# Queries and keys of the first four blocks as plain fp32 copies in a fused attention and MLP kernel on one Trainium2 core

## The chip, the core and the metric

The kernel runs on one core of a Trainium2 chip. A core has five engines that run their own instruction streams in order and wait for each other through semaphores: TensorE (PE, matrix products and transposes), VectorE (DVE), ScalarE (ACT), GpSimd (POOL) and SyncE (SP, which here only starts transfers). Sixteen DMA engines move data between main memory (HBM) and on-chip memory (SBUF). PE writes into PSUM, a small memory of eight banks, from which DVE or ACT must fetch the result. The metric is the device time of one execution in microseconds (us).

## What is computed

The first half is attention with four "sink" positions and a window of 128 positions; the second half is an MLP with a sigmoid gate on the attention's output. Shapes: 4 batches, 8 heads, 768 positions, 64 numbers per head; the MLP goes 512 to 2048 to 512 for 3072 tokens.

```
scores = scale * q @ k.T                         # per batch and head
keep   = (pos_k < 4) | (0 <= pos_q - pos_k < 128)
a      = softmax(where(keep, scores, -1e9))
x      = (a @ v) as (3072, 512)
h      = x @ w_in
out    = (h * sigmoid(1.702 * h)) @ w_out
```

## The kernel before, in words

The 3072 tokens are 24 blocks of 128 positions, six per batch. Blocks are worked in the order 0, 6, 12, 18 (the first block of every batch), then 1, 2, 3, 4, 5, 7 and so on. The number behind an operation's name is its block (or, for the MLP, its group: groups 0 and 1 are blocks 0 and 6 alone, group 2 is blocks 12 and 18, group 3 is blocks 1 and 2, and from there on two blocks each).

**Attention of a block.** `k0`, `q0`, `v0` load the block. For the first eight blocks q and k land as 128 rows of 512 numbers in the tile `qkn`. PE transposes them (`tk`, `tq`), DVE or ACT copies the result from PSUM into `qkT` (`ck`, `cq`). PE forms the scores in two PSUM tiles (`sc`; in the first block of a batch after a mask, `msk`, which is itself a product with the constant `identb`; in the others with the sink scores `snk`). DVE takes the row maxima (`mx`). In the first four blocks DVE negates them (`nb`) and ACT takes the exponential straight from PSUM (`bx`, eight instructions per block); in the others DVE masks and subtracts (`pk`, `sb`) and ACT takes the exponential from SBUF (`ex`). The result is transposed, for the first six blocks by PE (`ta`, fetched by `ca`) and from then on by a DMA transpose on SP's queue (`tat`); POOL cuts the window out of it (`sp`, `so`); PE multiplies with the values (`av`), DVE divides by the sums (`nm`). The block's output is transposed by PE (`tx`, fetched by `cx`) or by a DMA transpose (`txd`).

**MLP of a group.** `h3_0` to `h3_7` are the products with `w_in`, one PSUM tile each; the gate follows on ACT (`g`), or for groups 0 to 2 as a tanh on ACT (`th`) and a multiplication on DVE (`g`). `o1_0` to `o1_3` are the four quarters of the product with `w_out` for block 1; quarter n needs the n-th quarter `wo0` to `wo3` of `w_out`, as the n-th quarter of the `h` needs `wi0` to `wi3` of `w_in`. `ev` fetches and `st` stores the block's output.

**What sets the order.** Every operation is recorded with the engines that may run it, the operations it depends on and the buffers it takes and frees. The string `ORDER` then gives one order of all operations, by number; a letter behind a number picks the engine where there is a choice (d for DVE, a for ACT, p for POOL, s for SP). Each engine runs its operations in that order, one after the other, so an instruction that waits holds up everything behind it on its engine. Buffers are rings: `mm` (three PSUM tiles) serves `tk`, `tq`, `ta`, `tx`, `h` and `o`; `sc` (two PSUM tiles) one block's scores. A transfer carries a semaphore out of one of two rings of eight, one for transfers started by POOL and one for those started by SP and ACT together, and a transfer waits, on the engine that starts it, until the transfer that had the same semaphore eight places before it has landed.

**The transfers.** Before the change all q, k, v and weight loads are started by POOL (lines L286, L294, L263, L300, L307); these convert fp32 to fp16 on the way. SP and ACT start only the constants (L215), the four small loads `vsa0` to `vsa3` of the sink values (L315, used by `vsb0` to `vsb3`, L320), the DMA transposes and the stores. The tail of the kernel is block 23, whose output is split into 320 and 192 columns.

The beginning of each engine's order before the change:

```
PE   msk0 tk0 tq0 tk6 sc0 tk12 tq12 ta0_0 tq6 msk6 av0_0 ta0_1 sc6 tq2 av0_1 tk18 tx0 ta6_0 tq18 h0_3 ...
ACT  own bias0 later ck0 cq0 ck6 ck12 bx0_0 bx0_1 cq6 ca0_1 cq2 bx6_0 bx6_1 cq18 th0_3 ca6_1 th0_0 ...
DVE  zv zk z1 za1 za2 za3 zs za0 vsb0 vsb1 ks0 mx0_0 vsb3 nb0_0 mx0_1 nb0_1 cq12 ca0_0 ...
POOL k0 q0 k6 k12 v0 q12 q6 q2 wi3 k18 vsb2 v6 q18 wi0 wi1 k1 wi2 v12 wo0 wo1 q1 v18 wo2 wo3 k4 k2 q4 ...
SP   ident bias1 identb vsa0 vsa1 vsa2 vsa3 st0 st6 ...
```

Of the kernel before, what the change touches and what calls it, by code (L numbers as in the profile page):

```python
# [11 lines left out]
FP32 = mybir.dt.float32  # L12
# [7 lines left out]
P = 128  # L20
D = 64
# [3 lines left out]
PE, ACT, DVE, POOL, SP = "PE", "ACT", "DVE", "POOL", "SP"  # L25
BLOCKS = [0, 6, 12, 18] + [6 * s + r for s in range(4) for r in range(1, 6)]
# [4 lines left out]
TQ = {0, 6, 12, 18}  # L31
# [23 lines left out]
108 106 126a 99p 148 109 101d 149a 19 110 112 111 24 113 150 114 86 115 151d 127 88 116d 130 128a 152 26 129 119 117  # L55
90 120 131 118a 227 132 22 121 228a 135 133 122 171 87 134 136 123 172d 89 137 138 124d 173 27 139d 619 174a 175 153
25 620 142 621 140 154 143 141a 610 158 155 91 144 613 611 145 612 146 614 93 159 147d 194 160 156 615 631 195d 157
637 35 632 616 29 638 633 176 639 617 161 628 618 162a 36 634 629 177 630 635 163 181 622 164a 636 34 167 182 640 178
183 168 623 32 179 180 196 33 641 197d 165 184 166 198 38 185a 624 204 201 188 186 189 642 187a 28 625 190 169 626a
191 643 43 170a 627 199 192 644a 37 200 280 193d 225 645 281a 202 39 652 226a 205 40 282 653 230 203 658 31 283a 231  # L60
208 207 649 654 41 659 206 285 210 258 42 650 660 229 259a 651 256 209 232 211 257a 646 286 212a 233 215 261 647 655
213 235 216a 648 214 304 661 656 234 217 657 670 239 218 236 662 664 44 262 238 671 45 237 241 665 663 219 240 46 260
666 242 220 672 243a 263 221 266 244 246 667 222 247a 245 267 306 248 676 323 668 307 249 268 250 677 669 49 251 673
47 264 252 674a 48 678 265 675 269 253 284 270 223 287 254 224a 679 271 290 255a 288 344 680a 682 291 681 692 683 289
688 345 292 325 293 689 305 326 693 684 308 294 311 686 309 272 690 312 687 273 295 310 313 276 50 314 324 277 685 696
51 691 327 315 330 52 704 328 694 331 296 705 697 329 316 333 274 297 332 706 275 695 55 343 361 334 300 349 54 278
698 301 53 346 298 699 350 317 279a 335 347 707 318 299 700 708a 352 348 302 709 58 701 351 303a 56 353 722 702d 57
712 703 723 354 718 319 713 362 399 320 719 720 368 336 365 321 721 714 322 337 710 715 61 363 724 711 364 60 369 340
725 732 341 59 370 716 366 338 717 726 355 367 371 733 339 372 356 342 382 381 383 734 384 64 387 727 373 63 385 357
62 388 728 419 386 735 389 729 736a 390 358 391 742 737 730d 401 392 746 743 402 359 400 731 360 374 748 747 403 406  # L70
740 375 749 404 738 741 407 67 744 739 405 66 408 376 745 750 65 377 409 754 410 378 760 393 379 420 380 751 761 394
426 423 421 755 70 411 422 427 762 68 424 752 69 457 428 395 753 425 756 396 763 429 430 757 764d 439 412 765 766 758d
440 759 774 767 413 431 397 768 398 71 495 775 438 72 769 770 441 73 444 776 771 442 416 777 445 772 417 778 773 447
446 414 779 443 780 432 415 448 788 418 433 477 782 478 789 75 781 449 783 74 459 790 76 460 784 791 796 792a 458 793
797 800 461 450 464 798 801 462 451 794 514 799 465 806 79 463 795 466 802 77 807 467 468 454 78 476 455 810 482 479
452 803 811 469 483 785 453 480 434 786a 808 484 787 485 804 435 809 481 497 816 805 498 486 436 496 437 470 812 499
456 502 516 817 471 500 813 487 503 81 818 517 814a 82 505 501 474 815 819 504 80 475 506 830 820d 822 507 831 826 821
488 472 823 515 473 827 832 521 489 518 836 833 522 85 824 837 519 83 552 828 825 523 84 520 490 829 834 508 491 524
534 525 492 509 537 838 493 844 540 494 835 535 839 536 538 512 526 845 541 840 539 542 846 590 513 841 543 544 847
842d 510 843 527 848d 860 511 849 850 528 861 545 573 553 574 864 559 851 556 852 865 531 853 856 532 872 857 546 554  # L80
854 555 547 557 529 855 858 530 558 866 533 859 560 862 561 867 863 562 563 572 868 575 578 548 873 576 564 579 869
577 874 870a 580 892 871 581 549 582 875 893 583 550 876d 591 565 551 886 877 597 566 882 594 887 592 880 883 593 598
567 881 888 584 568 595 878 889 585 599 569 879 884 596 570 894 885 600 571 601 900 895 890 602 896 891 901 586 902
587 916 897 603 917 910 898a 604 588 899 911 912 589 903 913 906 904a 607 905 907 914 608 908 915 918 909 922 919 605
928 606 920 609 929 921 923 930 924 931 925 932a 946 933 926a 934 927 947 944 935 940 945 938 941 936 939 948 937 962
949 950 942 951 943 956 952 957 953 958 954a 963 959 955 964 960a 965 961 966a 967
"""


# [64 lines left out]
def kernel(  # L154
# [12 lines left out]
    Bsz, H, S, Dh = q.shape  # L167
# [20 lines left out]
    def sb(tag, shape, dt, name):  # L188
        return Buf(tag, lambda: work.tile(list(shape), dt, tag=tag, bufs=RING[tag], name=name))
# [20 lines left out]
    def queue(e):  # L210
        return nc.scalar if e == ACT else nc.sync
# [21 lines left out]
    def copy(e, dst, src, factor=1.0):  # L233
        if e == POOL:
            nc.gpsimd.tensor_copy(out=dst, in_=src)
        elif e == DVE and factor != 1.0:
            nc.vector.tensor_scalar(out=dst, in0=src, scalar1=factor, scalar2=None, op0=ALU.mult)
        elif e == DVE:
            nc.vector.tensor_copy(out=dst, in_=src)
        elif factor != 1.0:  # L240
            nc.scalar.mul(out=dst, in_=src, mul=factor)
        else:
            nc.scalar.copy(out=dst, in_=src)  # L243
# [8 lines left out]
    for unit in XUNITS:  # L252
        buf = sb("xn", (P, max(map(len, XUNITS)), H, D), FP16, f"xn{unit[0]}")
        for n, b in enumerate(unit):
            xunit[b] = (buf, n, unit)

    for pos, b in enumerate(BLOCKS):
        bb, r = divmod(b, 6)
        for w, src in (("k", k), ("q", q), ("v", v)):
            view = src[bb, :, r * P : (r + 1) * P, :].rearrange("h s d -> s h d")  # L260
            if w == "v":
                ld["v", b] = plan.add(
                    f"v{b}", POOL, 0.88, lambda b=b, view=view: nc.gpsimd.dma_start(v65[:, b, :, 0:D], view),  # L263
                    deps=[z_1], dma=("ld", LD), key=10 * pos - 45,
                )
            else:
                buf, n, unit = tunit[b]
                if b in HW:
# [583 lines left out]
```

## Time and profile before

| what | value |
|---|---|
| median of 3 runs | 234.83 us (234.34 to 236.19) |
| the profiled execution, whole | 235.92 us |
| its span, first to last instruction | 234.2 us |
| granted TensorE clock | 1.00 of full speed |
| PE busy | 218.3 us (93%) |
| DVE, ACT, POOL busy | 148.6, 146.1, 110.5 us |
| loads started by POOL | 13.64 MB as written, 66816 packets |
| first `h` product, last quarter of `w_out` in use | 19.70 us, 39.78 us |

The span leaves out 1.7 us of the execution's time. Busy time of PE is an upper bound of its work, because the ends of matmuls are modelled and a matmul that is held up inside the pipeline counts as busy. In the profile "L739" is line 739 of the kernel; a name such as `hT` is a tile. `PEld` is PE's load of weights, which runs beside the products. `ACTq` and `SPq` are the engines' queues for starting transfers.

### The profile page before, as it was taken

Reading aid. Unit: us, or ns where it says so; the run is one execution under the profiler, and the core shown is the slowest. Engines: PE = TensorE matmul, PEld = TensorE weight load, DVE = VectorE, ACT = ScalarE, POOL = GpSimd, SP = SyncE. Lnnn points to the kernel's source line nnn. Section 1 sums busy time; section 2 is a strip of 40 time slices with the busy share of each in tenths; the row PEclk is TensorE's granted clock in tenths of the full one; section 3 lists DMA queues with packets and bytes.
Section 4 is the critical chain, followed back from the end, with each engine's and each line's share of the span. In section 5 each row is a group of like instructions: output and inputs, shape, how many; then the busy total and the mean of one; then the engine's idle time right before and its main releaser. Section 6 shows DMA issues by size and latency. Waiting matters only on the chain.

```text
span 234.2 us, 5547 instructions
## 1 busy us (share of the span) xinstructions
PE 218.3 (93%) x2250; PEld 152.2 (65%) x2250; DVE 148.6 (63%) x384; ACT 146.1 (62%) x226; POOL 110.5 (47%) x129
## 2 busy tenths in 40 slices
PE   0778899999998999999999799999999999999994
PEld 0556865776585478576587486586586585775863
DVE  2587765899999967876966079869857782210000
ACT  2368663885599884477488368578474668351632
POOL 8594433966435958764950880838312060300000
PEclk9999999999999999999999999999999999999999
DMA  5999999999989999999999999699982534412202
GB/s 83 181 158 199 195 197 192 196 147 108 174 112 119 114 171 182 169 182 188 173 132 192 159 145 191 91 201 167 163 143 45 98 95 68 75 45 48 90 0 90
DMA packets 117832, 32.08 MB, mean 137 GB/s; under 512 B 108432, under 2 KB 114864, under 8 KB 117808
## 3 DMA queue, kind: packets, MB, share of 16 engines
q0 software_dynamic: 66816, 13.64, 69.6%
q1 hardware_dynamic: 50656, 18.00, 45.0%
q8 instruction: 17, 0.28, 0.5%
q10 hardware_dynamic: 336, 0.10, 0.2%
q14 instruction: 7, 0.06, 0.1%
HBM read 27.46 MB, written 6.29 MB: 144 GB/s over the span
## 4 chain that ended last, share of the span: by engine, by line
PE 63%; DVE 16%; DMA 16%; POOL 2%; issue 1%; SPq 0%; ACT 0%; DVEq 0%
PE hT L739 27%; PE o L789 27%; DMA w_out<-in_moe_w_out_dram 6%; DMA w_in<-in_moe_w_in_dram 4%; DVE mx L498 3%; DMA xT<-xn 3%; DVE e L535 3%; PE sc L436 3%; DVE sc L488 3%; DVE gT L760 2%; DMA vsa<-in_v_dram 2%; PE av L663 2%; PE av L665 2%; PE av L658 2%; DVE xn L676 1%; DVE mx L501 1%
## 5 line engine op out<-in xcount | busy, mean ns | idle before, releaser
L739 PE MATMUL hT<-xT,w_in 128*128 128x256 f16 (+1 forms) x832 | 93.2, 264 | 2.6 <-DMA xT<-xn 1.2
L789 PE MATMUL o<-w_out,gT 128*128 128x512 f16 (+2 forms) x400 | 91.9, 370 | 0.5 <-DMA w_out<-in_moe_w_out_dram 0.4
L739 PEld LDWEIGHTS <-w_in 128*128 128x128 f16 x832 | 73.8, 98 | 16.4 <-issue 4.3
L769 ACT ACTIVATE gT<-hT 128x512 f16<-128x512 f32 x80 | 46.5, 597 | 31.5 <-PE hT L739 31.3
L789 PEld LDWEIGHTS <-gT 128*128 128x128 f16 x400 | 36.4, 97 | 33.4 <-issue 1.9
L590 POOL TENSOR_SCALAR_AFFINE_SELECT atp<-at 128x1024 f16<-128x1024 f16 (+1 forms) x22 | 22.2, 1010 | 74.5 <-DMA at<-a 62.3
L498 DVE TENSOR_REDUCE mx<-sc 128x4 f32<-128x512 f32 x48 | 32.5, 681 | 0.1
L488 DVE COPY_PREDICATED sc<-later,sc 128x512 f32<-128x512 uint16 x40 | 26.0, 689 | 7.4 <-PE sc L436 7.1
L535 DVE TENSOR_TENSOR e<-sc,mx 128x512 f32<-128x512 f32 x40 | 26.3, 681 | 0.1
L675 DVE RECIPROCAL rcp<-av 128x4 f32<-128x4 f32 x48 | 8.5, 176 | 27.3 <-PE av L665 24.3
L559 ACT ACTIVATE a<-e 128x1056 f16<-128x1056 f32 (+2 forms) x24 | 22.5, 938 | 4.2 <-DVE rcp L675 1.6
L263 POOL DMA_DIRECT2D v<-in_v_dram x24 | 21.7, 906 | 6.1 <-DMA w_out<-in_moe_w_out_dram 3.3
L590 POOL TENSOR_SCALAR_AFFINE_SELECT at<-at 128x1024 f16<-128x1024 f16 (+1 forms) x22 | 22.2, 1010 | 1.5
L676 DVE TENSOR_TENSOR xn<-av,rcp 128x256 f16<-128x256 f32 x48 | 20.4, 424 | 1.7
L559 ACT ACT_TABLE_LOAD x13 | 16.7, 1283 | 5.7 <-issue 3.1
L769 ACT ACT_TABLE_LOAD x14 | 18.0, 1283 | 1.1 <-PE hT L739 0.5
L243 ACT COPY osb<-o 128x512 f32<-128x512 f32 (+2 forms) x13 | 7.2, 553 | 18.3 <-PE o L789 14.1
L663 PE MATMUL av<-v,at 128*128 128x65 f16 x192 | 17.5, 195 | 0.3 <-POOL at L590 0.3
L663 PEld LDWEIGHTS <-at 128*128 128x128 f16 x192 | 14.7, 99 | 4.1 <-POOL at L590 0.6
L294 POOL DMA_DIRECT2D qkn<-in_k_dram x16 | 14.4, 897 | 2.1 <-PE sc L436 2.1
L665 PE MATMUL av<-v,atp 128*128 128x65 f16 x160 | 15.1, 194 | 0.0
L294 POOL DMA_DIRECT2D qkn<-in_q_dram x16 | 14.3, 894 | 0.0
(54 smaller groups left out, 197.2 us busy)
## 6 DMA issues: line engine op xcount, KB each, us to landing
out_dram<-osb SPq DMA_DIRECT2D x23, 256.0 KB, 4.0
qkn<-in_k_dram POOLq DMA_DIRECT2D x24, 128.0 KB, 6.9
qkn<-in_q_dram POOLq DMA_DIRECT2D x24, 128.0 KB, 6.5
v<-in_v_dram POOLq DMA_DIRECT2D x24, 128.0 KB, 6.7
w_in<-in_moe_w_in_dram POOLq DMA_DIRECT2D x4, 512.0 KB, 9.1
w_out<-in_moe_w_out_dram POOLq DMA_DIRECT2D x4, 512.0 KB, 13.9
at<-a SPq DMA_TRANSPOSE x18, 5.2
qkT<-qkn SPq DMA_TRANSPOSE x10, 6.3
```

What stands on the lines that cost most here:

```text
L263: f"v{b}", POOL, 0.88, lambda b=b, view=view: nc.gpsimd.dma_start(v65[:, b, :, 0:D], view),
L294: lambda buf=buf, n=n, w=w, view=view: nc.gpsimd.dma_start(buf()[:, n, "qk".index(w)], view),
L488: nc.vector.copy_predicated(out=t()[:, :, :, own].rearrange("p l j s -> p (l j) s"), mask=later.unsqueeze(1).to_broadcast((P, 4, P)), data ...
L498: nc.vector.tensor_reduce(out=part, in_=t()[:, :, :, own], axis=AX.X, op=ALU.max)
L535: nc.vector.tensor_tensor(out=e32()[:, 512 * hf : 512 * hf + 512].rearrange("p (l j s) -> p l j s", l=2, j=2), in0=t()[:, :, :, own], in1= ...
L559: nc.scalar.activation(out=a16()[:, lo:hi], in_=e32()[:, lo:hi], func=AF.Exp, scale=scale)
L590: nc.gpsimd.affine_select(out=dst, in_=at()[:, lo : lo + num], pattern=[[0, num], [1 if own else -1, P]], compare_op=ALU.is_ge if own else ...
L663: nc.tensor.matmul(av()[:, i], at()[:, c], v65[:, b, h], start=(r == 0), stop=(r == 0))
L676: nc.vector.tensor_tensor(out=xn()[:, xi, 4 * hf : 4 * hf + 4].rearrange("p (j l) d -> p l j d", l=2), in0=av()[:, :, 0:D].rearrange("p (l ...
L739: nc.tensor.matmul(ht()[:, n].rearrange("p (n t) -> p n t", n=NT), w_in16[:, c, bass.ts(f, P)], t0()[:, i0 : i0 + NT, c], start=(c == 0), ...
L769: lambda fs=fs, gt=gt, ht=ht: nc.scalar.activation(out=gt()[:, fs[0] : fs[-1] + 1], in_=ht(), func=AF.Gelu_apprx_sigmoid),
L789: nc.tensor.matmul(po()[:, 0:width], gt()[:, F, bass.ts(t, P)], w_out16[:, F, c0 : c0 + width], start=(F == 0), stop=(F == NF - 1),)
```

## The change

Queries and keys of blocks 0, 6, 12 and 18 no longer come through POOL. Each of these eight loads becomes two operations. `rk6` (say) is a plain fp32 copy of the same 256 KB, started by SP or ACT, into a quarter of a tile of the ring `gt2` (two tiles, of which the MLP's groups 3 to 12 later hold their gates); `fk6` then converts it to fp16 into `qkn`, on DVE, ACT or POOL. The ring of `qkn` grows from four to seven tiles. The string `ORDER` is a new one, over 976 operations where there were 968.

```diff
+HW = {0,6,12,18}
+LH = 0.64
+RING = dict(RING,qkn=7)
 ORDER = """
-4a 8d 1s 14 2s 0a 6 7 5s 3a 11 15 12 13 9 10 94 17 96 20 16 98 100 107 21 18 102 95d 30 103a 104 97d 92 105a 125 23
...
+19a 13 5s 12 10 11 38 1s 9 21a 7 31s 8d 34 0a 14s 6 29a 94 106 16a 23 4s 20d 2a 104 133 100 26a 22d 24s 134d 3a 135 35
...
+    raws = {}
+    for n, b in enumerate(b for b in BLOCKS if b in HW):
+        if n % 2 == 0:
+            buf = sb("gt2", (P, 4, H * D), FP32, f"raw{n // 2}")
+        raws[b] = (buf, 2 * (n % 2))
...
+                    if b in HW:
+                        raw, ri = raws[b]
+                        ri += w == "k"
+                        o = plan.add(
+                            f"r{w}{b}", {SP: 0.6, ACT: 0.65}, 0,
+                            lambda e, raw=raw, ri=ri, view=view: queue(e).dma_start(raw()[:, ri], view),
+                            take=[raw], dma=("h", LH), key=10 * pos - 2000,
+                        )
+                        ld[w, b] = plan.add(
+                            f"f{w}{b}", {DVE: 0.4, ACT: 0.49, POOL: 0.9}, 0,
+                            lambda e, buf=buf, n=n, w=w, raw=raw, ri=ri: copy(
+                                e, buf()[:, n, "qk".index(w)].rearrange("p t d -> p (t d)"), raw()[:, ri]
+                            ),
+                            deps=[o], take=[buf], give=[raw], key=10 * pos - 500,
+                        )
+                        continue
```

The new order moves more than the eight loads. Block 6 now comes first; the beginning of each engine's order is

```
PE   tk6 tq6 msk6 tq18 sc6 tk0 tq2 tk18 tk1 tq0 ta6_1 msk0 ta6_0 sc0 tq12 av6_0 av6_1 tk12 ta0_1 tx6 msk12 ta0_0 sc12 h1_0
     av0_0 h1_3 tq1 av0_1 h1_2 ta12_0 snk1 msk18 tx0 sc18 h1_1 ta12_1 h0_2 av12_1 h0_0 h0_1 av12_0 o6_0 sc1 ta18_0 o6_1 tk2
     h0_3 snk2 o0_0 o6_2 o0_1 av18_0 sc2 ta1_1 o0_2 ta1_0 o6_3 o0_3 ...
ACT  rk6 rq6 bias0 rk18 rq0 bias1 rq12 later cq6 cq18 ck0 cq2 bx6_1 bx6_0 fq12 ca6_1 cq12 bx0_1 bx0_0 cx6 ca0_0 ca0_1 th1_0
     bx12_0 bx12_1 th1_3 th1_2 cx0 th1_1 bx18_1 th0_2 bx18_0 th0_0 th0_1 ca18_0 ck2 th0_3 ex1_1 ...
DVE  za3 za2 za0 za1 zs z1 zv zk fk6 fq6 ck6 fq18 fk0 ks6 fk18 mx6_1 mx6_0 nb6_1 fq0 nb6_0 ck1 ck18 cq0 ks18 ks0 ca6_0 mx0_1 ...
POOL q2 k1 wi0 v6 wi3 q1 v0 wi2 wi1 v12 vsb2 wo0 vsb1 k2 fk12 wo1 wo2 k3 v18 wo3 q3 k5 q4 k4 ...
SP   identb ident rq18 rk0 vsa2 own vsa1 rk12 vsa0 vsa3 st6 st0 ...
```

In this order the semaphores of SP's and ACT's transfers come round as follows: `vsa2` waits for `rk6`, `rq0` for `identb`, `bias1` for `rq18`, `rq12` for `rk0`, `rk12` for `bias0`, and `later`, the last transfer that ACT starts before its first computation, for `vsa2`. In the output of block 23 the wider part (320 columns) is now the last product.

More of the change, by code (lines that the diff above doesn't have):

```diff
@@ L58 @@
[L58 to L62, printed above, removed]
@@ new lines @@
+238 630 628 36 239 650 214 211 217 631 39 215 216 629 196 218 237 51 197 223 243 632 224a 240 48 219 244 651 220a 225
+241 633 652a 221 245 194 653 49 634a 264 246 195d 248 266 635 242 50 265a 198 290 267d 247 47 288 199 291a 177 268
+289d 42 249 178a 200 274 269 222 254 201a 250 270 45 255a 271 654 251a 275 256 660 655 272 252 672 226 661 656 253 227
+277 662 673 657 53 228 663 674 658 52 276 258 664 54 675 659 312 273 257 669 676 259 56 278 292 665 260 677 55 670 666
+279 261 57 671 678 667 298 293 262 668 679 263a 294 331 684 295 299 229 685 296 680 230 301 297 314 231 280 681 300
@@ new lines @@
+84 470 797 474 82 791 471 475 486 484 476 792 490 487 798 491 458 793 477 488 799 459 794a 492 493 804 795 489 800a 86
+494 444 801 808 85 445 522 805 812 87 462 504 495 463 813 802 478 809 507 510 442 803 806 479 443 824 807 89 460 814
+88 461 825 90 464 815 482 816 483 810 817 505 818 811 506 511 826 508 819 496 512 524 827 509 497 513 820 525 514 828d
+480 92 829 821 481 560 91 830 822d 93 842 831 515 838 500 823 839 523 501 843 834 529 526 498 835 840 530 836 527 841
+531 832 837 598 532 528 844 833 499 533 542 502 846 545 516 548 543 852 544 845 517 534 549 562 847 563 853 546 550
@@ new lines @@
+518 848 547 551 854 519 552 849 855 535 850d 553 866 856a 536 600 858 867 601 851 561 857 520 567 872 859 521 868 564
+873 568 554 537 869 862 565 555 864 569 863 570 538 860 865 566 539 861 870 540 571 880 541 581 874 582 871 881 572
+558 882 559 580 883 586 583 898 884a 587 573 556 885 899 584 886 557 574 890 887 585 892 589 891 588 875 590 900 876
+901 591 599 577 605 877 578 893 894 602 878a 606 575 879 895 888 603 896 607 889 592 604 902 897 576 593 908 608 579
+609 903 909 904 610 910 905 914 906a 596 907 915 920 597 611 911 921 594 912d 612 916 595 913 924 917 928 925 922 929
@@ L87 @@
+615 923 926 616 918 927 613 919 930 614 936 617 931 937 932 938 933 939 934a 954 935 940a 952 941 955 946 953 956 947
+944 957 948 945 942 949 950 943 958 951 964 959 965 970 960 971 961 972 962a 966 973 963 967 974a 975 968a 969
 """
@@ L267 @@
                 buf, n, unit = tunit[b]
-                if b in HW:
+                if b in HW and b not in TQ:
                     raw = const.tile([P, H, D], FP32, name=f"raw{w}{b}")
```

42 lines of the change are left out of this document (15 added, 27 removed).

## The prediction

> **What bounds the kernel now.** I read three views, from the whole to the place. First the table of windows, which gives each engine's busy time per stretch:
>
> ```profile
> 4.00:8.00 4.00, 2.46 (x52) 1.80 (x52) 0.12 (x1) 0.82 (x2) 3.98 (x6) 1.00 1.41 169
> 12.00:16.00 4.00, 3.05 (x32) 2.09 (x32) 2.98 (x11) 2.68 (x9) 4.00 (x6) 1.00 1.34 152
> 20.00:24.00 4.00, 3.19 (x56) 2.73 (x54) 2.61 (x8) 2.40 (x5) 0.92 (x1) 1.00 1.26 206
> 24.00:32.00 8.00, 7.64 (x137) 7.04 (x137) 5.50 (x12) 5.79 (x15) 3.31 (x5) 1.00 1.44 192
> 32.00:40.00 8.00, 7.55 (x73) 3.83 (x71) 5.50 (x14) 4.05 (x12) 3.03 (x4) 1.00 1.35 198
> 40.00:80.00 40.00, 38.87 (x455) 27.04 (x454) 37.38 (x94) 31.64 (x50) 26.41 (x32) 1.00 1.44 138
> 80.00:225.00 145.00, 143.76 (x1302) 99.78 (x1301) 85.72 (x224) 90.82 (x119) 61.40 (x63) 1.00 1.11 132
> ```
>
> The columns are the stretch, its length, PE, PEld, DVE, ACT, POOL, the clock, the DMA share and GB/s. From 24 us on PE is nearly full, so the end moves only with the moment at which PE gets going and with PE's later gaps. Between 40 and 80 us DVE is as full as PE. By the chain's pieces a quarter of `h` or `o` costs PE 0.87 us, a block's scores 0.54, a `tk` or `tq` 0.44, a `ta` 0.22 to 0.28, a `snk` 0.12. Adding up what PE did by these prices, it had done 11.6 us of work by 24 us, 25 by 40 and 63 by 80: it lost some 12 us before 24, 3 us up to 40 and 2.1 from 40 to 80. What matters is the way to the first `h`. The timeline shows it:
>
> ```profile
> 2.17 1.28 ACT L243 ACT_TABLE_LOAD   x1 [2.17 <-issue]
> 7.66 0.59 ACT L243 CAST qkT<-tq 128x512 f16<-128x512 f32 x1
> 7.88 1.53 DVE L320 TENSOR_TENSOR vsb<-vsa,ownm 32x520 f16<-32x520 f32 x2 [4.39 <-DMA vsa<-in_v_dram]
> 10.93 1.22 DVE L320 TENSOR_TENSOR vsb<-vsa,ownm 32x520 f16<-32x520 f32 x1 [0.54 <-DMA vsa<-in_v_dram]
> 12.53 2.18 ACT L521 ACTIVATE a<-sc,nb 128x128 f16<-128x128 f32 x8 [2.42 <-DVE nb L510]
> 17.96 2.18 ACT L521 ACTIVATE a<-sc,nb 128x128 f16<-128x128 f32 x8
> ```
>
> Each line is start, length, engine, instruction and, in brackets, the wait before it. ACT is free early (its table is loaded at 2.17), but DVE sits in front of `vsb` waiting for `vsa`, and the first exponential starts only at 12.53. Last, the chain of waits, in order of time:
>
> ```profile
> 24.89 14.85 DMA w_out<-in_moe_w_out_dram
> ...
> 126.41 7.43 DMA xT<-xn
> ```
>
> The last quarter of `w_out` lands at 39.78 and PE uses it at once, after 0.40 us of waiting: there PE and the weights run side by side. The second line holds PE's only later wait on a transfer, 1.24 us.
>
> **What is removed.** Eight POOL issues of 0.62 us (the row of L286), 5.0 us on POOL's queue. `wi0` moves from fifteenth to third place, `wi3` from ninth to fifth. So `w_in` should no longer be waited for (0.8 us of PE's waits). For `wo3` the bytes count: by 40 us the windows give 6.9 MB, fifteen block loads, the weights and some 0.7 MB of later ones. The new order has seventeen block loads ahead of `wo3`, 0.26 MB more, but starts at about 2 us and keeps eight larger transfers outstanding, so the dips to 169 and 152 GB/s should fill: 7.15 MB at 195 GB/s from 2 us on, `wo3` at 38.6. Raw copies write fp32, twice the bytes; all reads are the same, and I count them like the loads they replace (if written bytes set the rate, 1.05 MB more, 5.4 us; a rival below).
>
> **What is added.** Eight casts of 512 numbers a row: six on DVE, for which the trace has no row (between 0.22, the small memset of L225, and 0.69, a cast from PSUM; I take 0.42, the copy L239 of 512 fp16 numbers), one on ACT (0.59), one on POOL (between 0.64, a selection of 512, and 1.12). DVE's six, 2.5 us, stand before 14 us, where DVE is idle for more than half of the time; without that idleness they would cost the 2.5.
>
> Then the waits on ACT's queue, and here lies the price. ACT now starts five raw copies and three constants before its first computation, at 0.34 (a store of the same 256 KB) to 0.45 us each, about 3.3 us. The last, `later`, waits for `vsa2` to land, which is started only when `rk6` has landed. `rk6` starts at 0.81; a store of its size lands in 3.2 us (1.8 to 7.3): 4.0. `vsa` took 4.4 us from its issue to its use, the small `bias` 2.1: I take 4.2, near the row of the same transfer. So `vsa2` lands at 8.2 (4.7 to 12.5). Behind it stand `later` (0.45), the table load (1.28) and everything ACT does; `cq6` ends at 10.5, where ACT's second copy ended at 8.25 before.
>
> From there, step by step: `cq18`, `ck0`, `cq2` (0.59 each, `ck0` waiting for its transposes) to 13.1; two `bx6` of 1.09 to 15.3, which frees the score tiles; `msk0` 1.03, `ta6_0` 0.4 and `sc0` 0.6 to 17.3; two row maxima and the negation to 18.9; `bx0` 2.18 to 21.1; `cx6` 0.59, and `msk12`, `ta0_0`, `sc12` on PE, to the first `h` at **22.5**, against 19.70. The second block's exponentials end at 21.1 against 20.1. After that the new order is ahead: `w_in` is there, ACT has 12.7 us of listed work from `cx6` to `th0_3`, and block 1's exponential follows at about 35, against 45.2.
>
> **The sum.** From the first `h` to the last `w_out` quarters the new order holds 17.6 us of PE work, the old 17.4, which took 20.1. With `w_in` early I take 1.2 us of gaps (0 to 2.7): 22.5 + 18.8 = 41.3, later than `wo3` (38.6), so the weights are not the bound. Against 39.78 that is 1.5 us later, but by then 1.5 us more of PE's work is done (`sc2` 0.54, a net `tk` 0.44, two `snk` 0.24, a net `ta` 0.28). So **0.0** up to here (-1.2 to +1.5 by the gaps alone). From 40 to 80 PE lost 2.1 us beside a full DVE. DVE now has the softmax of blocks 1 and 2 behind it: -1.3 (0 to -2.1). From 80 on nothing of the change is left but the order. Between a block's last `av` and its group's first `h` the old order leaves at least 7.2 us of PE work at the place of the 1.24 us wait, and about as much (6.9 to 7.3) at three others without one; the new one leaves 5.9 at block 8 and 6.2 at block 19. I count the same 1.2 (0 to 3): 0. The tail evicts 320 columns instead of 192 (0.43 against 0.32) and stores more: +0.2. In all -1.1: 235.92 becomes 234.8 for the profiled execution. The median is 1.09 below that execution, so 233.7, and within 1%, which is about what a measurement of this kernel can tell from no change.
>
> **Rivals.** *Early release, faster.* If `vsa2` lands as fast as `bias`, at 5.5, everything behind moves up by 2.7 us, the first `h` to 19.8, and the last quarters to 38.6, where `wo3` takes over: 231.0. For it speaks that few transfers compete before 4 us; against it that `rq18` and `rk0` are queued ahead of `vsa2` on SP.
>
> *ACT held, slower.* If `vsa2` lands at 12 the first `h` comes at 26.3, and neither the weights nor DVE's lead cover it: 233.7 + 3.8 = 237.5. It decides from about 11.7 on (3.5 us later than assumed is 1% over the median). For it speak the 7.3 us of the slowest store and three queues sharing the engines; against it the 4.4 of `vsa` itself, beside full queues.
>
> *Written bytes.* If the fp32 copies run at the GB/s of the row, `wo3` lands at 44.0, 2.7 after PE wants it: 236.4. The transfers' reads speak against it.
>
> *Casts against POOL's issues.* `vsb` took 0.69 alone and 1.22 beside POOL's own `vsb`. If each DVE cast costs a POOL issue the same 0.53, the weights come 3.2 us later, at 41.8, 0.5 after they are needed: 234.2. The Trainium skill ("SBUF — State Buffer", section "SBUF: two separate sides") says that an fp32 copy by VectorE within SBUF shuts GpSimd out of their shared port, so that it can't write descriptors until the copy ends; by that rule the casts would hold up just the weights that the change brings forward. The two `vsb` rows agree with it, though the trace has no such copy beside an issue.
>
> **How the numbers follow.** Forecast 0.42, early release 0.28, ACT held 0.19, written bytes 0.07, casts 0.04. Of the forecast's own spread (231.5 to 236.5, by the gaps, DVE's lead and the steady order) 0.02 lies under 232.5; of written bytes with a late stall 0.05 lies over 237.2. So faster 0.30, same 0.46, slower 0.24. The forecast's own range does not hold enough; reaching to 231.0 with its gaps (-0.7) and to 237.5 with a stall of 0.7 gives 230.3 to 238.2.
>
> **What would show it.** First exponential (L546 in the new file) near 13.1; ACT's table load near 8.7 behind its transfers; first `h` near 22.5; last `w_out` quarters near 41; block 1's exponential before 37; DVE less than 90% busy between 45 and 80; no PE wait on `w_in`. A table load before 7 or after 11 makes the number wrong, and so do new PE waits on `xT` at groups 6 and 10.

## The result and the profile after

The changed kernel takes **252.36 us** (median of six runs, 250.28 to 253.91); the kernel before, run beside it on the same chip, takes 235.58 us (234.34 to 236.19). The ratio is 1.0715, with a 95% interval of 1.0654 to 1.0775: slower by 16.8 us. Here and below, ratios and their intervals leave out disturbed executions, those more than 1.5% above the fastest of the same kernel, so that a ratio can differ from the quotient of the medians beside it. The forecast was 233.7 us, and its range ended at 238.2. The profiled execution of the changed kernel took 250.28 us with a span of 248.5, against 235.92 and 234.2 before: 14.3 us more span.

The table of windows of the changed kernel, in the stretches that the prediction showed (columns as there: stretch, length, PE, PEld, DVE, ACT, POOL, clock, DMA share, GB/s):

```profile
4.00:8.00 4.00, 0.64 (x16) 0.51 (x16) 0.43 (x1) 0.00 (x0) 4.00 (x6) 1.00 1.03 195
12.00:16.00 4.00, 2.22 (x36) 1.51 (x36) 1.60 (x4) 0.00 (x0) 0.00 (x0) 1.00 1.34 225
20.00:24.00 4.00, 3.62 (x85) 3.09 (x82) 3.85 (x12) 3.15 (x10) 1.10 (x1) 1.00 1.14 215
24.00:32.00 8.00, 5.93 (x96) 4.81 (x95) 6.70 (x17) 5.43 (x14) 3.70 (x6) 0.79 1.05 150
32.00:40.00 8.00, 7.61 (x143) 6.80 (x141) 7.50 (x22) 6.48 (x19) 3.54 (x5) 1.00 1.30 170
40.00:80.00 40.00, 37.69 (x436) 25.54 (x434) 38.23 (x87) 24.84 (x46) 24.52 (x30) 1.00 1.45 146
80.00:225.00 145.00, 140.18 (x1299) 96.10 (x1298) 96.46 (x241) 96.07 (x123) 64.82 (x67) 1.00 1.09 131
```

PE's work is the same (219.0 us busy against 218.3), so the loss is PE's idle time. Over the first 40 us PE is busy 20.89 us, against 29.46 before: 8.6 us lost. From 40 to 80 it loses 1.2 us more than before, from 80 to 225 another 3.6. With 0.7 us more of busy time these make 14.1 of the 14.3 us.

The timeline of the changed kernel shows where the start went (start, length, engine, instruction, and in brackets the wait before it):

```profile
5.83 0.43 DVE L242 CAST qkn<-raw 128x512 f16<-128x512 f32 x1 [2.34 <-DMA raw<-in_k_dram]
12.38 0.43 DVE L242 CAST qkn<-raw 128x512 f16<-128x512 f32 x1 [6.12 <-DMA raw<-in_q_dram]
...
5.88 0.70 SPq L340 DMA_DIRECT2D vsa<-in_v_dram  x1
...
15.76 0.62 ACTq L298 DMA_DIRECT2D raw<-in_q_dram  x1
16.84 0.32 ACTq L218 DMA_DIRECT2D later<-clater  x1
17.20 1.28 ACT L246 ACT_TABLE_LOAD   x1 [17.20 <-DMA bias<-cbias]
...
21.31 2.19 ACT L546 ACTIVATE a<-sc,nb 128x128 f16<-128x128 f32 x8
...
31.03 1.07 PE L764 MATMUL hT<-xT,w_in 128*128 128x128 f16 x16
```

The first two rows are the first casts, `fk6` and `fq6`. `rk6` landed after 5 us, `rq6`, started 1.2 us later (2.04), only at 12.38. `vsa2` (8 KB) started at 5.88, as soon as `rk6` was there, and `later`, which waits for it, at 16.84. ACT, which began to load its table at 2.17 before, does so at 17.20, behind its own transfers. The first exponential starts at 21.31 instead of 12.53, the first `h` at 31.03 instead of 19.70.

The chain of waits names the transfers (start, length, piece):

```profile
2.73 13.00 DMA raw<-in_k_dram
15.76 9.50 DMA raw<-in_q_dram
25.29 0.63 ACT qkn L246
...
82.69 9.17 DMA qkT<-qkn
```

A raw copy of 256 KB (`rk0`) takes 13 us; `rq12`, which waits for `rk0` because of the ring of eight semaphores, another 9.5; its cast is what PE waits for. The chain before had one DMA transpose in it, the changed one six, of which one is shown.

The DMA queues of the changed kernel between 6 and 14 us (packets, MB written, share of the 16 engines; q0 is POOL's, q1 and q10 carry SP's and ACT's transfers):

```profile
q0 software_dynamic: 1943, 0.93, 86.7%
q1 hardware_dynamic: 290, 0.53, 24.0%
q10 hardware_dynamic: 313, 0.36, 17.8%
```

The shares add up to more than 100%: the engines have work throughout. POOL, which has started all four quarters of `w_in` by 8.2 us, keeps 116 GB/s as written and twice that as read; the copies, which are wanted first, get 66 and 45 GB/s together with the small loads of their queues.

### The profile page after: what moved, and what is told of

It is laid out like the page before. It is cut to its first block, busy times and chain, and to the rows that moved or that the text cites. A ratio compares the mean times of both kernels' runs of the same rounds, so it can differ in the third digit from the quotient of the medians.

```text
span 248.5 us, 5553 instructions
## 1 busy us (share of the span) xinstructions
PE 219.0 (88%) x2250; PEld 152.4 (61%) x2250; DVE 158.6 (64%) x391; ACT 145.6 (59%) x225; POOL 107.6 (43%) x123
## 4 chain that ended last, share of the span: by engine, by line
PE 42%; DMA 25%; DVE 18%; POOL 5%; ACT 3%; SPq 3%; issue 2%; POOLq 0%; ACTq 0%
PE o L814 18%; PE hT L764 18%; DMA at<-a 12%; DMA raw<-in_k_dram 5%; DMA raw<-in_q_dram 4%; DMA qkT<-qkn 4%; DVE mx L523 4%; DVE gT L785 3%; DVE sc L513 3%; POOL atp L615 2%; DVE mx L526 2%; DVE e L560 2%; DVE xn L701 2%; SPq L407 2%; POOL at L615 2%
## 5 line engine op out<-in xcount | busy, mean ns | idle before, releaser
L814 PE MATMUL o<-w_out,gT 128*128 128x512 f16 (+2 forms) x400 | 90.3, 371 | 0.0
L794 ACT ACTIVATE gT<-hT 128x512 f16<-128x512 f32 x80 | 46.3, 597 | 26.4 <-PE hT L764 25.8
L246 ACT COPY osb<-o 128x512 f32<-128x512 f32 (+2 forms) x16 | 9.0, 559 | 20.9 <-PE o L814 19.5
L688 PEld LDWEIGHTS <-at 128*128 128x128 f16 x192 | 14.2, 98 | 5.4 <-POOL at L615 2.0
L384 PEld LDWEIGHTS <-qkn 128*64 128x64 f16 x256 | 6.7, 135 | 15.4 <-DVE qkn L242 12.5
L526 DVE TENSOR_TENSOR mx<-mx,ms 128x4 f32<-128x4 f32 x40 | 15.0, 376 | 1.4
## 6 DMA issues: line engine op xcount, KB each, us to landing
w_out<-in_moe_w_out_dram POOLq DMA_DIRECT2D x4, 512.0 KB, 14.3
```

The lines of the kernel that those rows point to most:

```text
L526: nc.vector.tensor_tensor(out=part, in0=part, in1=ms[:, 4 * hf : 4 * hf + 4], op=ALU.max)
L688: nc.tensor.matmul(av()[:, i], at()[:, c], v65[:, b, h], start=(r == 0), stop=(r == 0))
L794: lambda fs=fs, gt=gt, ht=ht: nc.scalar.activation(out=gt()[:, fs[0] : fs[-1] + 1], in_=ht(), func=AF.Gelu_apprx_sigmoid),
L814: nc.tensor.matmul(po()[:, 0:width], gt()[:, F, bass.ts(t, P)], w_out16[:, F, c0 : c0 + width], start=(F == 0), stop=(F == NF - 1),)
```

## The experiments

The question was which of four things costs the 16.8 us: the copies as such, the queues of SP and ACT, the held queue of ACT, or the new order. Each run stood beside runs of the kernel before on its chip (236.08 to 236.43 us in these groups).

### One part alone: the copies in the old order

```diff
 the order of before, ring of seven
-POOL k0 q0 k6 k12 ... q12 q6 ... k18 ... q18
+SP   rk0 rq0 rk6 rk12 rq12 rq6 rk18 rq18 at the same places of ORDER
+DVE  fk0 ... each just ahead of its transposes tk0 ...
```

> The old order, with the eight loads as plain fp32 copies started by SP alone and cast by DVE, ring of seven; ACT starts only its three constants, as before. If the fp32 copies themselves are the cause (twice the written bytes at some 215 GB/s, and starved beside POOL's queue): 240 to 246 us, first h after 24 us. If the new order or ACT's held queue is the cause: 233 to 238 us, ACT's table load near 2.2 and first h within 1.5 us of 19.7.

Measured: 245.4 and 251.69 us in two runs, so no interval, but 9 us or more above the 236.15 beside them. ACT loads its table at 2.17 here, as before the change, and still, in the longer of the two, the first exponential starts at 18.55 and the first `h` at 29.3. So 9 of the 16.8 us or more need neither the held ACT nor the new order: the copies on SP's queue, with their casts, make them.

### One part alone: the new order with converting loads

```diff
-HW = {0,6,12,18}
+HW = set()
-rk6.a ... rk12.s, fk6.d ... fk12.p
+POOL k6 q2 q6 q18 k1 k0 k18 wi0 q0 v6 wi3 q12 k12 ...
```

> The new order, but the eight loads go through POOL again, converting on the way, each at the place where its plain copy was started; no casts, ring of seven. If the copies and the waits on their semaphores are the cause: 233 to 238 us, first h by 22 us. If the new order is the cause (weights ahead, later stalls): 245 to 253 us.

Measured: 242.62 us, ratio 1.0278 (1.0206 to 1.0349), between the two expectations. The groups of PE's waits up to 40 us:

```profile
PE tk L385 <- DMA qkn<-in_k_dram: 6.1, 1, 6.1
PE tq L385 <- DMA qkn<-in_q_dram: 5.1, 3, 3.0
```

The first is the usual wait for the first load. The second are `q` loads that this order puts behind others on POOL (`q0` stands behind `wi0`), though PE wants them first. An order made for eight loads on other queues is not the order for POOL's queue, so this run overstates what the order costs. The runs in need order, below, mend that.

### The held ACT

```diff
-bias1.a rq12.a later.a
+bias1.s rq12.s later.s
```

> The changed kernel, with the three transfers that hold ACT (bias1, rq12, later) started by SP instead. If ACT's hold is the cause of most of the loss: table load near 5, first exponential before 17, 240 to 246 us. If the copies land too late anyway (q6 was cast at 12.4): table load near 5, first exponential only 2 to 4 us earlier than 21.3, 248 to 251 us.

Measured: 253.9 us, ratio 1.0755 (1.0651 to 1.086): nothing gained, although ACT loads its table at 5.15 us; the first exponential starts at 20.28, only 1.0 us earlier. The chain of this run:

```profile
3.70 14.09 DMA raw<-in_k_dram
...
18.17 9.76 DMA vsa<-in_v_dram
```

Now an 8 KB load takes nearly 10 us and is waited for by the sums of `vsb`. Freeing ACT moves the wait; the transfers behind it are as late as ever.

### The copies with the DMA engines to themselves

```diff
-SP   rq18 rk0 vsa2 own vsa1 rk12 ...
+SP   rq18 rk0 rk12 vsa2 own vsa1 ...
-POOL q2 k1 wi0 v6 ...
+POOL fk12 q2 k1 wi0 v6 ...
```

> The changed kernel, with the copy rk12 moved ahead and its cast by POOL put first on POOL, so that POOL starts no load before seven of the copies have been queued and rk12 has landed: the copies run alone. If POOL's traffic starves them: six of them land within 8 us (0.7 us each if the bytes read set the pace, 1.2 us each if the bytes written do), first exponential before 15, and the weights come 6 to 9 us later; 244 to 252 us. If they are slow by themselves: POOL's first load not before 14 us, 255 us or more.

`fk12` waits for `rk12`, so POOL starts nothing until 13.46 us. Measured: 250.13 us, ratio 1.0596 (1.0421 to 1.077). That lies within the first expectation, but not by its mechanism: the first exponential starts at 19.68, not before 15. The windows of this run, in the stretch in which the copies are nearly alone:

```profile
4.00:14.00 10.00, 2.85 (x52) 2.01 (x52) 2.88 (x8) 0.22 (x1) 0.54 (x1) 1.00 0.56 192
```

The copies land sooner (`fq6` at 8.52 instead of 12.38), but two queues together carry 192 GB/s, with the engines busy 0.56 of the time. At this rate the 2.1 MB of the eight copies take 11 us. In the run with block 12 ahead, further down, where nearly all the traffic is POOL's converting loads, 197 GB/s are written between 6 and 14 us; by these two rates eight loads of half the size take half the time, an estimate. The weights, started at 15.38 instead of 2.69, and ACT's table load, which still waits for the transfers ahead of it (13.78), take the gain away: the first `h` starts at 30.1.

### The small sums later, in the kernel before

```diff
-DVE  vsb0 vsb1 ks0 mx0_0 vsb3 nb0_0 mx0_1 nb0_1 ...
+DVE  vsb0 vsb1 ks0 mx0_0 nb0_0 mx0_1 nb0_1 vsb3 ...
-POOL ... k18 vsb2 v6 q18 wi0 wi1 k1 wi2 v12 wo0 wo1 q1 ...
+POOL ... k18 v6 q18 wi0 wi1 k1 wi2 v12 wo0 wo1 vsb2 q1 ...
```

> The kernel before, with two operations moved: the second half of the own-value tables (vsb3 on VectorE) stands behind nb0_1 instead of ahead of it, and vsb2 on GpSimd behind wo1 instead of ahead of v6. Nothing is left out. If the waits for vsa at 8 to 12 us are what holds the first exponential (12.53 us) and GpSimd's issues, the first exponential comes 1 to 2 us earlier, and the time is 233.5 to 235.0. If the arrival of the queries and keys and GpSimd's own issues set the start, the first h stays at 19.7 and the time at 235.2 to 236.3.

Measured: median 236.47 against 236.31; ratio 0.9948 (0.9908 to 0.9988). That is a gain of half a percent, 0.9 at most, and not by the theory: the first exponential starts at 12.35 instead of 12.53, the first `h` at 19.97. PE now waits 1.45 us for a key load ahead of that, and the row maxima come no earlier.

### The old start with the new order behind it

```diff
 ORDER: the first 205 operations of the old order, then the changed order's remaining operations; loads by POOL
```

> The first 205 operations stand as in the kernel before (until about 40 us), the others in the changed kernel's order; GpSimd loads all queries and keys, the ring is seven. It tells what the changed order costs behind the start. After 40 us PE idles 2.4 us in the kernel before, 7.1 in the changed one and 4.4 in the changed order with GpSimd's loads. If the later order costs by itself, 237.5 to 239.5, with PE's pauses at xT and av again. If what that kernel lost lies in the start (the pause of PE and the half clock behind it), 235.2 to 236.5.

Measured: 247.28 us, ratio 1.0494 (1.0443 to 1.0545), far above both expectations. The windows:

```profile
40.00:60.00 20.00, 14.01 (x203) 10.54 (x202) 15.64 (x39) 11.39 (x24) 13.68 (x19) 0.83 1.39 122
```

PE stands still for 6 us just behind the seam, with pauses for DVE's subtraction, for ACT's copies and for `qkT`, and then runs at half clock for a while. The second order counts on work being done by the seam that the first has not done there; that this is the whole of the pause was not tested. The run prices the seam, not the order, and says nothing on the question.

### The loads in need order

```diff
-POOL k6 q2 q6 q18 k1 k0 k18 wi0 q0 v6 ...
+POOL k6 q6 q18 k0 q2 k18 k1 q0 wi0 v6 ...
```

> The changed order with GpSimd loading all queries and keys as in the run of the new order, but the eight loads stand first, as PE needs them (k6 q6 q18 k0 q2 k18 k1 q0), ahead of wi0. If the start of that run (first h at 23.6, half clock from 19 to 25.6 us) came from q0 behind wi0, the first h comes by 21, there is no half clock before 30 us, and the time is 238 to 240.5. If the order costs all of it later on, the time stays at 242 to 243 with an earlier first h.

Measured: 239.77 us, ratio 1.0138 (1.0097 to 1.0179): 2.9 us less than in the order of the copies. The time lies within the first expectation, but partly by luck: the half clock is there, and the first `h` stays at 23.36, because of one more wait, in the timeline:

```profile
17.90 0.64 PE L385 MATMUL tq<-ident,qkn 128*64 128x64 f16 x16 [4.01 <-DMA qkn<-in_q_dram]
```

That is `tq12`; `q12` stands behind `wi0` and a second quarter of `w_in` on POOL.

### The row size

```diff
-raw()[:, ri]                             <- 128 rows of 2 KB
+raw()[0:64 or 64:128, both quarters]     <- 64 rows of 4 KB
```

> As the run with the raw copies first, but each copy goes to 64 partitions in rows of 4 KB instead of 128 rows of 2 KB (keys in the upper half of the partitions, queries in the lower one), and each cast takes 64 partitions x 1024. The bytes are the same; which element is where is not, so the scores of these four blocks are computed from permuted rows: that part of the output is another, the work is of the same size but for the casts, 0.8 us instead of 0.42. If a price by the row limits the copies (both queues carried 181 to 201 GB/s together, with the DMA engines busy 55 percent), the rate goes to 300 GB/s or more between 4 and 10 us, the first exponential comes 3 to 5 us earlier (19.68 there), and the time is 244 to 247.5. If the bytes limit it, the rate stays near 190 GB/s, and the time is 249.5 to 252.

Measured: 253.74 us, ratio 1.0737 (1.07 to 1.0775), against 250.13 for the kernel that it was built on, the one with the copies first. The windows:

```profile
4.00:14.00 10.00, 2.08 (x36) 1.44 (x36) 3.68 (x7) 0.00 (x0) 0.00 (x0) 1.00 0.54 138
```

138 GB/s instead of 192, with the engines as busy as before. A price by the row would have raised the rate, and a limit by bytes kept it, so both expectations fail. Half the partitions per copy, or fewer and larger pieces, made it slower; which of the two was not told apart. What limits the copies alone stays open.

### The same copies, started by GpSimd

```diff
-ACT rk6 rq6 rk18 rq0 rq12   SP rq18 rk0 rk12
+POOL rk6 rq6 rq18 rk0 q2 rk18 k1 rq0 wi0 v6 ... rq12 rk12 ...
 casts as in the changed kernel
```

> The changed kernel, but all eight raw fp32 copies are issued by GpSimd, in the order in which PE needs them (as in the run in need order), and cast as in the changed kernel; SP's and ACT's queues keep only the constants and the small sums. Nothing is left out. Against the run in need order (239.77 us) it has the copies' bytes and the casts in place of converting loads. If SP's and ACT's queues are the cause (slow, and holding the small transfers), the copies land at GpSimd's rate, about 0.65 us apart, the first exponential comes by 16, the first h by 23, and the time is 239 to 243. If plain fp32 copies and casts are dear whoever issues them (twice the written bytes, at 190 GB/s as before), the first h stays at 28 or later and the time at 246 to 252.

Measured: 246.17 us, ratio 1.0456 (1.0385 to 1.0527). The time is just within the second expectation: 6.2 us better than the changed kernel, 6.4 worse than the converting loads in nearly the same order. The first exponential starts at 14.04, as the first theory had it, but the first `h` at 29.79, as the second had it. The timeline says why:

```profile
22.92 0.62 ACT L247 CAST qkn<-raw 128x512 f16<-128x512 f32 x1 [6.35 <-DMA raw<-in_q_dram]
```

`fq12` waits for `rq12`, which lands at 22.9, where `q12` landed at 17.9 in the run with the loads in need order.

### The small transfers first

```diff
+ACT identb bias0 bias1, SP ident vsa2 own vsa1 later vsa0 vsa3, then
 ACT rk6 rq18 rk18 rq12, SP rq6 rk0 rq0 rk12
```

> The changed kernel, but SP and ACT issue the ten constants and small sums ahead of the eight raw copies, so that no copy stands eight places ahead of one of them (each transfer of these two queues waits for the one eight places before it). Nothing is left out. If the held small transfers and ACT's held queue are what costs (table load at 17.2 us, vsa at 16.8), the table load comes by 8, the first h by 25, and the time falls to 242 to 245. If the copies' own landing sets it (the later ones landed at 18.2 and 25.3 us beside GpSimd's loads), the first h stays at 28 to 31, and the time at 248 to 253.

Measured: 256.61 us, ratio 1.0775 (1.0688 to 1.0862). No small transfer waits for a copy any more, and the time is no better than the changed kernel's; the first `h`, at 35.37, is later than in either expectation. The timeline of DVE:

```profile
10.46 0.43 DVE L243 CAST qkn<-raw 128x512 f16<-128x512 f32 x1 [6.97 <-DMA raw<-in_k_dram]
19.33 0.43 DVE L243 CAST qkn<-raw 128x512 f16<-128x512 f32 x1 [8.44 <-DMA raw<-in_q_dram]
```

The copies, started 1.4 us (`rk6`) and 4.1 us (`rq6`) later than in the changed kernel, land 4.6 and 7 us later. POOL's queue is full of weights by then. With the run of the held ACT this settles the held queues: they shape the start, but letting them go gains nothing as long as the copies land late.

### One block alone

```diff
-POOL k6 q6 q18 k0 ...
+ACT rk6, SP rq6 first; POOL q18 k0 ...
```

> As the run in need order (239.77 us), but the key and query of block 6 alone come as raw copies, the first thing that ACT's and SP's queues issue, and are cast on VectorE; GpSimd starts with q18. Nothing is left out. If the price is in proportion to the copies, a quarter of the 12.6 us between that run and the changed kernel: 242 to 244. If the price comes from copies that queue behind each other and hold the small transfers, two of them cost nearly nothing, and with two issues less on GpSimd (1.3 us) the time is 238 to 240.5.

Measured: 242.85 us, ratio 1.0302 (1.0255 to 1.0349): 3.1 us for two copies. That is the time of the first expectation, but not its cause: `fk6` starts at 5.4, and `fq6` waits for no transfer. The timeline of PE:

```profile
8.86 0.64 PE L385 MATMUL tk<-ident,qkn 128*64 128x64 f16 x16 [8.86 <-DMA ident<-cident]
10.62 0.64 PE L385 MATMUL tq<-ident,qkn 128*64 128x64 f16 x16 [1.12 <-DVE qkn L243]
```

`ident`, 32 KB, was started on SP at 2.36 behind `rq6` and landed at 8.86; PE's first product starts 2.9 us later than in need order (6.01), and the second 4.2 later, because its cast stands behind `ck6` on DVE. But the first `h` comes only 1.3 us later (24.62), as PE then waits 1.5 us for `q12` instead of 4.0. Where the rest of the 3.1 us arises was not followed up.

### The ring alone

```diff
+RING = dict(RING,qkn=7)
```

> The kernel before with the ring of seven buffers for the loaded keys and queries, and nothing else. The loads of the first blocks start without a wait for a buffer either way (four buffers hold the first four blocks), so both theories expect no change: 235.2 to 236.6. Below 234.5 the ring would be a gain that the change hides, above 237.5 a part of its loss.

Measured: 236.69 us, ratio 1.0009 (0.9963 to 1.0054). The ring does nothing that could be measured.

### What the order costs, and what a copy costs

Three last runs. The first takes the pause of 4.0 us away:

```diff
-POOL ... k1 q0 wi0 v6 wi3 q12 k12 ...
+POOL ... k1 q0 q12 k12 wi0 v6 wi3 ...
```

> As the run in need order (239.77 us), but GpSimd also loads q12 and k12 ahead of wi0. Nothing is left out. If the changed order costs its 3.5 us through PE's pause of 4.0 us ahead of tq12 and the half clock behind it, the pause goes, the clock stays at 1.00 to 40 us, and the time is 235 to 237. If its cost lies after 40 us (PE idles 2.1 us more there than in the kernel before, 2.0 of them at xT between 100 and 120 us), or if wi0, now two loads later, holds the first h instead, the time stays at 238 to 241.

Measured: 237.97 us, ratio 1.0045 (0.9992 to 1.0099). So the changed order, with its loads in the order in which PE needs them, costs about 1 us, and no difference lies inside the interval. Neither expectation holds: the time is between them, and the clock did not stay at 1.00. The pause ahead of `tq12` is gone, and half clock comes all the same in the profiled execution, from 16.0 to about 22.8 us (the clock is the third number from the end):

```profile
16.00:18.00 2.00, 0.45 (x6) 0.31 (x6) 1.64 (x6) 1.12 (x4) 1.94 (x3) 0.50 1.37 195
```

The longest pause of PE since its first product is 1.81 us here, the one ahead of `av` in the first of the two rows further down. The second run keeps the pause of 4.0 us and fills it:

```diff
+84 x matmul(tq12's tile, ident[:, 0:64], ident) ahead of tq12's own
```

> As the run in need order, but 84 more matmuls (64x64, of the unit matrix with itself, into the tile that tq12 overwrites) stand on PE ahead of the matmuls of tq12 that wait for q12. They fill some 2.5 to 3.3 us of the 4.0 us pause and compute nothing that is used. If the half clock from 16.8 to 24 us follows from PE's pause, it is gone, and 7.2 us at one half become 3.6: the time is 236 to 238. If the half clock has another cause, it stays, and the time stays at 239 to 241.

Measured: 238.35 us, ratio 1.0089 (1.0053 to 1.0125). The added products ran for 2.85 us from 13.70 on, the half clock came nevertheless, from 19.2 to 26.4 us instead of 16.8 to 24, behind the shorter pauses that were left. So the pause of 4.0 us is not needed for it; what sets it off isn't answered. The third run is the counterpart of the first, with copies for loads:

```diff
-POOL k6 q6 q18 k0 q2 k18 k1 q0 q12 k12 wi0 ...
+POOL rk6 rq6 rq18 rk0 q2 rk18 k1 rq0 rq12 rk12 wi0 ..., casts as in the changed kernel
```

> As the run with the copies by GpSimd (246.17 us), but the copies of block 12 also stand ahead of wi0. Nothing is left out. The difference to the run with block 12's loads ahead is the price of copies and casts alone, with no other queue and no weights ahead of them. If the copies' twofold written bytes and the casts cost by themselves, it is 4 us or more (eight copies at 0.87 to 1.3 us instead of 0.65 are 1.8 to 5.2 us of the DMA engines, and PE waits for a cast behind each). If the 6.4 us came from the copies of block 12 behind wi0 and wi1 (PE waited 5.1 us for fq12), it is below 3 us.

Measured: 241.26, 244.91, 245.0 and 248.89 us, without an interval. So the price of copies and casts is known only roughly: 7.0 us by the medians (244.96 against 237.97), 4.0 by the lowest of the four against 237.29, the median of the executions that the ratio of the run with loads rests on. In the two profiled executions PE is busy 29.73 us up to 40 us with loads and 23.75 with copies, and the first `h` starts at 21.60 and at 29.04. As whole times these two (243.37 and 244.91) differ by only 1.5 us, since the one with loads lost more later: from 80 to 225 us PE idles 6.0 us in it, 2.7 in the other. Two rows of PE's timeline show what the copies displace, first with loads, then with copies:

```profile
16.72 0.38 PE L689 MATMUL av<-v,at 128*128 128x65 f16 x4 [1.81 <-DMA v<-in_v_dram]
```

```profile
23.37 0.28 PE L689 MATMUL av<-v,at 128*128 128x65 f16 x4 [3.13 <-DMA v<-in_v_dram]
```

`v6` is the same converting load in both kernels and needs no cast. It lands 6.7 us later, and eight transfers ahead of it write 1.05 MB more: by its landing 3.85 MB have been written instead of 2.57. At the 197 GB/s of the converting loads the 1.05 MB are 5.3 us, an estimate; and POOL starts `v6` 1.4 us later, since it waits for the landing of earlier copies in its ring of eight semaphores. Written bytes are the nearer measure but not an exact one, since in the stretch in which the copies made most of the traffic more was written per us than by converting loads (the last number, GB/s):

```profile
4.00:6.00 2.00, 0.00 (x0) 0.00 (x0) 0.00 (x0) 0.00 (x0) 2.00 (x4) 1.00 1.01 264
```

## Why the prediction was wrong, point by point

**The sum of the runs.** By their ratios, one thing added after the other: the order with loads in need order +0.0045, copies and casts for loads, with block 12's copies behind `w_in`, +0.041, SP's and ACT's queues for POOL's +0.026. Together 0.0715, of 235.58 us: 1.1, 9.7 and 6.1 us, each uncertain by 1 to 2 us. The ring is nothing. The run with all copies ahead, which has no interval, splits the 9.7 us: eight copies and casts are 7.4 and the place of block 12's copies 2.2 by its median, 4.1 and 5.6 by its lowest execution, 241.26 us (a ratio of 1.0217).

**The step that failed: "I count them like the loads they replace".** The prediction had both readings. All reads are the same, or written bytes set the rate; it took the first and gave the second a chance of 0.07 and a price of 5.4 us, of which the weights' slack was to hide half (236.4). The runs speak for written bytes: behind copies `v6` comes 6.7 us later, and eight copies in place of eight loads, at the same places of POOL's order and with the casts that they need, cost 4 to 7 us. The 5.4 us were of the right size; that nothing or only half of them would show was wrong. The slack was counted for the wrong transfer: it was the weights' slack, while `rq12`, `v6` and the other early transfers, which PE wants one after the other, have none (in the changed kernel the first `h`, behind them, is 11.3 us later).

**A second half of the same step: three queues are not three times the room.** The prediction took `rk6` from the row of a store, 3.2 us, and `vsa2` from near its own row, 4.2. They took 5 and 11. Both rows came from moments in which the queue had little ahead of it. From 6 to 14 us all engines had work, and the early transfers shared them with POOL's weights. The profile before showed the warning: 178 GB/s and a DMA share of 1.32 between 4 and 14 us, with almost nothing beside POOL's loads. The prediction named "three queues sharing the engines" in the rival "ACT held", but let it delay one transfer of 8 KB instead of all of them. And the two queues are slow even without POOL's weights: at the 192 GB/s of the run with the copies first, the eight copies take 11 us.

Of the issuing queue the Trainium skill ("DMA: Bandwidth & Descriptors", section "Issuing engine by pattern") says that SP's and ACT's way is generally the faster, and names SP for simple loads. Here the same copies were 6.2 us better on POOL's queue (252.36 against 246.17). Two things differ, and no run parts them: there most of them stood ahead of the weights and not beside them, and between 4 and 6 us 255 GB/s were written, where SP's and ACT's queues brought 189 in the run with the copies first. The Trainium skill ("DMA: Bandwidth & Descriptors", section "Queues, rings and completion order") has each DMA engine take the queues in turn; the 0.93, 0.53 and 0.36 MB above agree with it so far as each queue kept a share, whatever was urgent.

**ACT's queue.** The mechanism was right: `later` waits for `vsa2`, and the table load for `later`. The sizes were off: table load at 17.20 against 8.7, first exponential at 21.31 against 13.1, first `h` at 31.03 against 22.5. The prediction's own mark, a table load after 11, was passed. ACT's issues of raw copies took 0.60 to 1.21 us, not 0.34 to 0.45. What it did not price is the wait of `rq12` for `rk0`, though the list of semaphores ahead of it has that wait; it is the chain's second piece. And the run of the held ACT shows that a free ACT would have been worth nothing.

**The casts** were sized right: 0.42 to 0.43 us for five of DVE's six, 0.62 on ACT and on POOL, against 0.42, 0.59 and 0.64 to 1.12. The sixth took 1.26 us, from 18.19 on, beside POOL's `vsb` (18.04 to 19.16), as the `vsb` on DVE had taken 1.22 beside POOL's. That they hold up POOL's issues, the rival at 0.04, has one trace: in the run with copies by GpSimd an issue of POOL waited 0.33 us for a DVE cast to end.

**The removed issues.** `w_in` is not waited for any more, as forecast (`wi0` stood fourteenth on POOL, not fifteenth; nothing hangs on it). That gained nothing, since the first `h` waits for its input. POOL's freed time was lost again: `vsb2` held it for 7.5 us, until 18.04, for `own`, the transfer behind `vsa2`.

**From 40 us on.** Forecast was -1.3 from 40 to 80 and nothing later. It became +1.2 and +3.6. DVE's lead never came: block 1's exponential starts at 46.61, against 35 in the forecast and 45.18 before, and DVE is busy 38.23 of 40 us. After 80 us PE waits at `xT` (1.9 us; new waits there were one of the prediction's signs against itself), `qkT` (1.0) and POOL's window cut (1.3). The run in need order, without copies, already idles 2.3 us more there than the kernel before, so most of that belongs to the order, as far as one profile of each can tell. The prediction took PE's idle time there at 1.2 us, as before, with a range of 0 to 3; it is 4.8.

**The range.** Bytes and shared queues were two rivals with a price each (236.4 and 237.5). They are one thing in one place, the transfers of the first 30 us, and the range took in the larger of them instead of their sum. Even the sum, 2.7 and 3.8 us on 233.7, is 240.2, still 12 us short: neither price held the delay of all early transfers.

## What to carry to other kernels

When loads move to idle queues, count the bytes that they write and the DMA engines that all queues share. Here an idle queue was no idle bandwidth, and the queue with the weights in it took its part from the transfers that were wanted first. An urgent transfer belongs ahead of the bulk on the same queue, as the converting loads in need order were (ratio 1.0045, against 1.0715 for plain copies on two more queues). And a duration taken from a quiet moment of the trace is no price for a moment at which the change adds traffic.

## What the runs showed of the hardware

- Two queues of SP and ACT, nearly alone, carried 192 GB/s of fp32 copies in rows of 2 KB, with the DMA engines busy 0.56 of the time, and 138 GB/s in rows of 4 KB on half the partitions. Started by POOL, the same copies in rows of 2 KB were written at 255 and 264 GB/s between 4 and 6 us, with two converting loads among them. POOL's converting loads wrote 197 GB/s and, at four bytes read for two written, read twice that. Why the copies of SP and ACT don't fill the engines is open.
- Small transfers can take as long as large ones beside full queues: 32 KB took 6.5 us behind one copy, 8 KB 9.8 and 11 us, against 4.4 for 8 KB in the kernel before.
- The granted clock falls to one half in some of the starts: in the changed kernel from 27.3 to 30.8 us (0.52), in need order from 16.8 to 24 (0.53), with the pause filled from 19.2 to 26.4 (0.55), with block 12 ahead from 16.0 to 18 and on (0.50), and not at all in the profiled kernel before. The Trainium skill ("TensorE: Matmul & The Clock Gate", section "HAM oscillation — how this bites in real kernels") tells of half clock behind idle gaps of more than 3.4 us. The 4.0 us ahead of `tq12` fit that. Others do not: with block 12 ahead the longest pause is 1.81 us, and in the changed kernel pauses of 5.91 us (up to 12.86) and 3.34 us (up to 19.13) passed with the clock at 1.00. So the length of one pause does not tell here; what does is open.
